# Keeping K and V whole, ordering the loads one by one, and fixing the norm engines in a one-core transformer block

## The chip, the cores and the metric

The kernel runs on one core of one Trainium2 chip. The metric is the device time of one execution in microseconds (us). For a program on one core a run further than 1.5% above the fastest of its kernel counts as slow.

The engines are named as the profile names them: PE is TensorE (matmuls), PEld its weight loads, DVE VectorE, ACT ScalarE, POOL GpSimd, and SP the engine that issues the transfers. "PEclk" is the clock granted to PE as a share of full speed.

## The reference, cut to what matters

A block with conditioning: six modulation vectors come from a small vector `c`, local attention (A) follows a normalization, and a token-mixing MLP (B) follows a second and a third one. S = 2048 tokens, D = 512, 32 heads of 16, a window of 8 keys with dilation 2, F = 1792, all in bf16.

```python
mod = (_silu(c) @ w_mod).reshape(c.shape[0], 6, 1, -1)      # sa, ca, ga, sb, cb, gb
h = _layernorm(x) * (1 + ca) + sa
x = x + ga * _A_ref(h, wqkv, wo)   # q.k over idx = pos - 2*w, w = 0..7; softmax; sum of attn*v; @ wo
h = _layernorm(x) * (1 + cb) + sb
x = x + gb * _B_ref(h, w1, b1, w2, b2)
# _B_ref: h = layernorm(x); u = gelu(einsum('bsd,sf->bdf', h, w1) + b1); y = einsum('bdf,fs->bds', u, w2) + b2
```

## The kernel before

The tokens are split into 16 tiles of 128, and the tiles into five chunks of 2, 4, 4, 4 and 2 tiles (chunks 0 to 4). Each chunk passes through statistics (DVE), normalization, a transpose, the Q, K and V projections (PE), the products Q*K (DVE) with their reduction by matmuls (PE), a softmax, the products with V (DVE), the output projection, two more norms, and then its part of the first MLP matmul. When the last chunk is through, the MLP is finished in a long run of matmuls.

A small scheduler in Python decides the order. Every piece of work is added to a graph with an estimated duration, a rank, and one or more possible engines; the scheduler simulates the engines and emits the instructions in the order of its simulated starts. Because a proxy issues them all, every instruction has the same source line in the profile: L208 in the kernel before, L238 in the changed one. The reader goes by the tile names in the rows.

```python
k_r = ring(NB, [P, 4 * (PAD + CM)], BF, "k_c")     # K of two chunks; PAD = 16 columns are the halo
v_r = ring(NB, [P, 4 * (PAD + CM)], BF, "v_c")
...
if ch:                                             # the halo of K and V is copied from the chunk before
    pC = SIZES[ch - 1] * P
    for nm, cur, r in (("k", k_c, k_r), ("v", v_c, v_r)):
        prev = r[(ch - 1) % NB][:, 0:4 * (PAD + pC)].rearrange("p (j s) -> p j s", j=4)
        copy2(cur[:, :, 0:PAD], lambda prev=prev: prev[:, :, pC:pC + PAD], 4 * PAD, True, ...)
...
# a norm: the scheduler chooses DVE or ACT; the tiles of POOLN1 = (2, 3, 4, 10, 11, 12, 13) go to GpSimd
alts = [("dve", 0.42, lambda: nc.vector.tensor_scalar(dst, src, r_, n_, op0=ALU.mult, op1=ALU.add)),
        ("act", 0.8, lambda: nc.scalar.activation(dst, src, ACT.Identity, scale=r_, bias=n_))]
if pool:
    alts = [("pool", 0.8 if st < 6 else 2.0, lambda: nc.gpsimd.tensor_scalar(...))]
...
# output projection of one tile: the residual x is added by a fifth matmul, with the identity
for dq in range(4):
    nc.tensor.matmul(ps(s_), lhsT=o_sb[:, dq, ...], rhs=woq[:, dq, :], start=(dq == 0), stop=False)
nc.tensor.matmul(ps(s_), lhsT=ident[:], rhs=xx[:, st, :], start=False, stop=True)
...
# products Q*K of one quarter of the head dimension, and their reduction into psL
nc.vector.tensor_tensor(prod, qv, kv, op=ALU.mult)
nc.tensor.matmul(psL[...], lhsT=group4[:], rhs=prod()[...], ...)
```

## Time and profile before

The median was 218.91 us over three runs (218.16 to 219.75), and the profiled execution spans 216.9 us.

| Stage of the kernel before | Time | PE busy | What limits it |
|---|---|---|---|
| 8.00 to 27.09 us | 19.09 us | 11.48 us | loads, GpSimd's norms, VectorE |
| 27.09 to 213.25 us | 186.16 us | 181.67 us | PE itself |

The profile's page of the kernel before, engine totals (busy us, share of the span, instructions) and two rows of its 40 slices (each digit is the busy share of a slice in tenths):

```profile
PE 199.7 (92%) x1450; PEld 99.4 (46%) x1474; DVE 170.1 (78%) x264; ACT 125.9 (58%) x276; POOL 25.9 (12%) x39
...
PE   7776599999999999799998999999999999999993
...
POOL 6025501994000000000000000000000000000000
```

Only the first five slices of PE, and the last, are far from full. In the rest, PE is nearly always busy, so a gain must come from the front, from fewer matmuls, or from the few gaps that are left.

The waits of PE in the kernel before (who was waited for, us in total, times, longest):

```profile
PE psS L208 <- POOL h L208: 2.7, 1, 2.7
PE psS L208 <- DMA wst<-in_w_mod_dram: 1.9, 1, 1.9
PE psS L208 <- DMA h<-in_A_wqkv_dram: 1.6, 1, 1.6
PE psS L208 <- DMA wst<-in_A_wqkv_dram: 1.4, 1, 1.4
```

The timeline of PE in the kernel before, from the last matmuls of chunk 0's projections to chunk 1's first projection (start, us, instruction, count, and in brackets the idle time before it and what ended it):

```profile
14.90 3.66 PE L208 MATMUL psS<-hT,w_qkv 128*128 128x256 bf16 x32
20.41 1.04 PE L208 MATMUL psS<-wst,sc_rep 128*128 128x512 bf16 x3 [1.85 <-DMA wst<-in_w_mod_dram]
...
21.93 0.29 PE L208 MATMUL psS<-ident,h 128*128 128x128 bf16 x2
24.88 0.96 PE L208 MATMUL psS<-ident,h 128*128 128x128 bf16 x14 [2.66 <-POOL h L208]
25.77 0.62 PE L208 MATMUL psL<-big,group 128*32 128x512 bf16 x8
...
27.09 1.03 PE L208 MATMUL psS<-hT,w_qkv 128*128 128x512 bf16 x4
```

The rows `psS<-ident,h` are chunk 1's transposes; they need chunk 1's norms. The row at 27.09 us is chunk 1's first projection (512 columns; chunk 0's have 256), from which on PE is all but full. The same norms on GpSimd, from the timeline of POOL in the kernel before:

```profile
18.45 6.37 POOL L208 TENSOR_SCALAR h<-xx,rs,nb 128x512 bf16<-128x512 bf16 x3 [2.52 <-DVE nb L208]
```

Three norms take 6.37 us there, to 24.8 us (2.73, 0.76 and 2.91 us one by one), and the transposes follow at 24.88. The windows of the kernel before (start:end, length, then busy us and instructions by engine, granted PE clock, share and rate of the transfers):

```profile
8.00:27.09 19.09, 11.48 (x145) 9.02 (x143) 13.84 (x30) 9.76 (x24) 7.83 (x5) 1.00 0.99 299
27.09:213.25 186.16, 181.67 (x1222) 84.03 (x1242) 152.59 (x224) 112.75 (x247) 14.34 (x4) 1.00 0.72 142
```

### The profile page before, as it was taken

How to read it: one execution, taken by the hardware profiler on the slowest of the kernel's cores; microseconds unless marked ns; L12 is line 12 of the kernel's file. 1: busy time of each engine (PE TensorE's matmuls, PEld its weight loads, DVE VectorE, ACT ScalarE, POOL GpSimd, SP SyncE). 2: the span in 40 equal slices, each digit the busy share in tenths (PEclk: the TensorE clock that was granted, in tenths of full speed). 3: DMA queues.
4: the chain of work that ended last, by engine and by line, in shares of the span. 5: the costliest groups of instructions: out<-in, count | busy, mean ns of one | idle time of the engine just before them, and what ended most of it. 6: DMA issues, size and time to landing. Idle time of an engine off the chain costs nothing.

```text
span 216.9 us, 3882 instructions
## 1 busy us (share of the span) xinstructions
PE 199.7 (92%) x1450; PEld 99.4 (46%) x1474; DVE 170.1 (78%) x264; ACT 125.9 (58%) x276; POOL 25.9 (12%) x39
## 2 busy tenths in 40 slices
PE   7776599999999999799998999999999999999993
PEld 7764344445444437433443333444444444444452
DVE  3579599999999899999999989998853455445553
ACT  3637489867897969988887757978753000000000
POOL 6025501994000000000000000000000000000000
PEclk9999999999999999999999999999999999999999
DMA  6999734499999999999989771997169201111111
GB/s 191 350 350 284 232 90 101 79 328 125 165 135 128 136 134 209 154 151 171 188 173 313 225 204 47 284 294 201 50 172 227 66 33 48 53 48 36 36 48 50
DMA packets 53127, 34.24 MB, mean 158 GB/s; under 512 B 18421, under 2 KB 52597, under 8 KB 53109
## 3 DMA queue, kind: packets, MB, share of 16 engines
q1 hardware_dynamic: 53100, 34.00, 72.7%
q8 instruction: 11, 0.18, 0.4%
q14 instruction: 8, 0.06, 0.1%
q10 hardware_dynamic: 8, 0.00, 0.0%
HBM read 22.03 MB, written 2.10 MB: 111 GB/s over the span
## 4 chain that ended last, share of the span: by engine, by line
PE 50%; DMA 14%; issue 8%; POOL 8%; SPq 6%; DVE 6%; ACT 4%; POOLq 2%; ACTq 0%
PE psS L208 50%; POOL h L208 7%; DMA vD<-v_c 7%; SPq L208 6%; DMA h<-in_A_wqkv_dram 5%; DVE big L208 3%; DMA wst<-in_B_w_dram 3%; POOLq L1028 2%; DVE h L208 2%; DVE st L208 1%; ACT junk L208 1%; ACT h L208 1%; ACT k_c L208 0%; ACT o_sb L208 0%; DVE mv L208 0%
## 5 line engine op out<-in xcount | busy, mean ns | idle before, releaser
L208 PE MATMUL psS<-h,wst 128*128 128x512 bf16 x216 | 51.5, 379 | 1.4 <-DMA wst<-in_B_w_dram 0.9
L208 PEld LDWEIGHTS <-wst 128*128 128x128 bf16 x324 | 30.1, 99 | 36.3 <-issue 2.0
L208 PE MATMUL psS<-hT,w_qkv 128*128 128x512 bf16 (+1 forms) x233 | 44.9, 337 | 0.4
L208 PEld LDWEIGHTS <-w_qkv 128*128 128x128 bf16 x282 | 29.6, 112 | 21.0 <-issue 3.8
L208 DVE TENSOR_TENSOR big<-q_sb,k_c 128x4096 bf16<-128x4096 bf16 (+1 forms) x20 | 37.6, 1894 | 0.5 <-PE psL L208 0.5
L208 DVE TENSOR_TENSOR big<-a2sb,vD 128x4096 bf16<-128x4096 bf16 (+1 forms) x20 | 36.8, 1860 | 0.2
L208 DVE SCALAR_TENSOR_TENSOR h<-psS,bcol,gb_bc 128x512 f32<-128x512 f32 (+1 forms) x17 | 12.2, 720 | 24.6 <-PE psS L208 23.0
L208 POOL TENSOR_SCALAR h<-xx,rs,nb 128x512 bf16<-128x512 bf16 x7 | 20.7, 2968 | 14.6 <-DVE nb L208 14.6
L208 ACT ACTIVATE h<-xx,nb,rs 128x512 bf16<-128x512 bf16 x25 | 19.4, 807 | 0.3 <-DVE nb L208 0.2
L208 DVE BATCH_NORM_STATS2 st<-xx 128x6 f32<-128x512 bf16 x24 | 16.3, 679 | 3.3 <-DMA xx<-in_A_x_dram 3.3
L208 PE MATMUL psS<-gT,big 128*128 128x512 bf16 x83 | 18.2, 379 | 0.1
L208 PE MATMUL psS<-woq,o_sb 128*128 128x512 bf16 x62 | 16.6, 381 | 0.9 <-ACT o_sb L208 0.8
L208 PE MATMUL psS<-gT,wst 128*128 128x512 bf16 (+1 forms) x82 | 15.2, 343 | 0.1
L208 PEld LDWEIGHTS <-ident 128*128 128x128 bf16 (+1 forms) x145 | 11.6, 113 | 7.4 <-issue 1.9
L208 ACT ACTIVATE gT<-psS 128x512 bf16<-128x512 f32 x22 | 12.1, 593 | 2.7 <-PE psS L208 2.7
L208 PEld LDWEIGHTS <-big 128*128 128x128 bf16 x116 | 9.1, 97 | 9.9
L208 ACT ACTIVATE k_c<-psS 128x512 bf16<-128x512 f32 x16 | 9.6, 598 | 6.5 <-PE psS L208 6.5
L208 DVE TENSOR_TENSOR psS<-psS,gT 128x512 f32<-128x512 f32 x14 | 9.2, 696 | 5.1 <-PE psS L208 5.1
L208 ACT ACTIVATE q_sb<-psS,qvb 128x512 bf16<-128x512 f32 (+1 forms) x20 | 11.7, 607 | 1.2 <-PE psS L208 1.2
L208 ACT ACTIVATE gT<-psS,bcol 128x512 bf16<-128x512 f32 x14 | 9.1, 687 | 5.2 <-DVE psS L208 5.2
L208 ACT ACTIVATE v_c<-psS,qvb 128x512 bf16<-128x512 f32 (+1 forms) x20 | 11.2, 619 | 1.0 <-PE psS L208 0.8
L208 DVE TENSOR_TENSOR h<-h,xx 128x512 bf16<-128x512 f32 (+1 forms) x17 | 11.2, 661 | 0.6
(94 smaller groups left out, 218.4 us busy)
## 6 DMA issues: line engine op xcount, KB each, us to landing
vD<-v_c SPq DMA_DIRECT2D x48, 130.0 KB, 7.5
wst<-in_B_w_dram SPq DMA_DIRECT2D x6, 768.0 KB, 5.3
wst<-in_B_w_dram SPq DMA_DIRECT2D x4, 896.0 KB, 6.7
big<-in_B_w_dram SPq DMA_DIRECT2D x3, 896.0 KB, 7.7
vD<-v_c SPq DMA_DIRECT2D x32, 66.0 KB, 3.5
out_dram<-h SPq DMA_DIRECT2D x15, 128.0 KB, 1.7
xx<-in_A_x_dram SPq DMA_DIRECT2D x3, 512.0 KB, 9.1
gT<-in_w_mod_dram SPq DMA_DIRECT2D x1, 1536.0 KB
```

Source lines behind the costliest of these rows:

```text
L208: r = fn(*a, **k)
L1028: with _tile.TileContext(nc) as tc:
```

## The change

The change has four intents: to have no halo copies (K and V are kept whole, so the halo is simply the columns to the left), to give every load its own rank so that the order follows need, to give every norm of every tile a fixed engine, and to take three residual adds from PE. The scheduler's model was refined too (GpSimd is blocked while VectorE holds a lock, transfers have a latency and a limited queue), which moves many starts.

```diff
-    k_r = ring(NB, [P, 4 * (PAD + CM)], BF, "k_c")
-    v_r = ring(NB, [P, 4 * (PAD + CM)], BF, "v_c")
+    k_f = T([P, 4, PAD + S], BF, "k_f")
+    v_f = T([P, 4, PAD + S], BF, "v_f")
...
-    POOLN1=(2, 3, 4, 10, 11, 12, 13),
-    LN2D=(2, 3, 10, 11, 12, 13, 14, 15),
+    NE=('AADADAPPPAAPPPAP', 'AAAAADDADAPDPAAA', 'DADDDDDDAAAAPDPD'),
+    X1D=(10, 11, 15),
+    LN2D=(10, 11, 12, 14, 15),
...
-    ld_w(1)
-    ld_w(0)
-    ld_x(1)
-    ld_w(2)
+    for t in (1, 0, 2):
+        G.pk = float(R[f"w{t}"])
+        ld_w(t)
+    for ch in range(1, NCH):
+        G.pk = float(R[f"x{ch}"])
+        ld_x(ch)
...
-    dma(rowA, wmod_view[:, :, 3 * D:6 * D], 3 * D * D * 2, [], ["rowA"], "ld_wmod345")
+    for r in range(3):
+        G.pk = float(R[f"wm{r + 3}"])
+        dma(rowA[:, :, r * D:(r + 1) * D], wmod_view[:, :, (r + 3) * D:(r + 4) * D], ..., f"ld_wmod{r + 3}")
...
-        if ch:                                     # the halo copies
-            ...
-                copy2(cur[:, :, 0:PAD], lambda prev=prev: prev[:, :, pC:pC + PAD], 4 * PAD, True, ...)
...
-                nc.tensor.matmul(ps(s_), lhsT=ident[:], rhs=xx[:, st, :], start=False, stop=True)
+                if st not in X1D:
+                    nc.tensor.matmul(ps(s_), lhsT=ident[:], rhs=xx[:, st, :], start=False, stop=True)
+            if st in X1D:
+                add("dve", 0.69, lambda st=st, s_=s_: nc.vector.tensor_tensor(xx[:, st, :], ps(s_), xx[:, st, :], op=ALU.add), ...)
```

In `NE`, each string is one of the three norms, each letter a tile: A is ScalarE, D VectorE, P GpSimd. The lists of instructions of both kernels, compared engine by engine, give: identity matmuls of the residual 16 to 13; x statistics on VectorE 24 to 21; parking casts of the MLP's partial sums on VectorE 6 to 0 and on ScalarE 22 to 28; halo copies on ScalarE 8 to 0; norms on ScalarE 30 to 22 and on GpSimd 7 to 11. The loads now go out in the order x of chunk 0, K's weights, x of chunk 1, the two first blocks of w_mod, V's weights, Q's weights, and the rest; before, both w_mod blocks and K's and Q's weights preceded the x of chunk 1.

## The prediction

> **What bounds it now.** The profiled span is 216.9 us, TensorE (PE) busy 199.7, VectorE 170.1, ScalarE 125.9 (engine totals). The PE timeline splits in two. From 27.1 to 213.3 us PE is all but full: about 3 us idle (gaps at 72, 90 to 92.5, 97 and 117 us). Before 27.1 us it is starved: between 8 and 27 us it is busy 11.5 of 19 us (windows view). The waits view names the causes: GpSimd's norm of chunk 1 (PE 2.7 us; ScalarE waits 3.2 us for the transposes behind it), the loads of w_mod (1.9), of V's weights (1.6) and of Q's (1.4). VectorE is over 95% busy from 30 to 118 us, nearly a second bound; in the last 67 us it is half idle.
>
> **What the change does.**
> 1. Chunk 1's norms leave GpSimd, where three tiles took 6.4 us (18.4 to 24.8 us); two go to ScalarE (0.8 us each), two to VectorE (0.4). The load of x for chunk 1 comes before both w_mod blocks. Chunk 1's transposes should run near 15 us, not 21.9 to 25.8.
> 2. Q's weights come last of the three, about 14 us instead of 10, and five more x statistics (0.8 us each) stand ahead of the first Q*K product on VectorE. I put it at 19 to 20 us (now 17.05). The four products then run without the 2.3 us wait for the maximum.
> 3. PE starts chunk 1's projections at about 25 us instead of 27.1, with two more modulation rows (0.95 us each) done: a lead of 3.5 to 4 us.
> 4. Eight halo copies of 0.26 us go from ScalarE. The instruction lists also show three statistics fewer on VectorE (0.8 each), six parking casts moved to ScalarE (0.67 on VectorE, 0.6 on ScalarE), three residual adds moved from PE (0.216 each, 0.65 in all) to VectorE (0.69 each). VectorE and ScalarE each lose about 3 us after 27 us.
> 5. GpSimd gets 11 norms instead of 7. The Trainium skill ("SBUF — State Buffer", Who interferes with whom) says that a VectorE operation with two SBUF inputs blocks a GpSimd operation reading SBUF; the trace agrees: a norm took 0.76 us at best, 5.97 at worst. Chunks 2 and 3 have room for it; the last tiles could hold the final h3.
>
> **On the critical path:** item 3 whole (PE-bound after it), 0.65 us of matmuls, perhaps 0.5 us of the 3 us idle. ScalarE's and VectorE's 3 us are mostly slack that keeps PE fed. Sum: about 5.2 us.
>
> **Prediction:** 213.7 us, 8 in 10 between 210.0 and 217.5. Faster by over 2% 0.57, within 2% 0.39, slower by over 2% 0.04.
>
> **What would show it.** In the PE timeline, chunk 1's first 512-column projection at 24 to 26 us (27.1 now); no PE wait for GpSimd's norm in the first 30 us; the first Q*K product at 18 to 20.5 us; PE idle under 4 us from there to the last matmul. No halo copies on ScalarE; the tail from the last level's matmuls unchanged, about 68 us.
>
> **What would make it wrong.** Slower: loads landing later than counted (a modulation row between the Q*K reductions then holds PE and psL); GpSimd norms of chunk 2 or of tiles 10, 12, 14 on the critical path; only 3 groups of matmuls follow the last output projection (12 before), so its norms may stall PE before the last level. Faster: Q's weights landing at 12 to 13 us, the 3 us of idle vanishing, or VectorE's relief counting fully, towards 210.

## The result, and the profile after

The changed kernel took 215.92 us (median of 4 runs, 215.62 to 216.15) against 218.86 for the kernel before (4 runs, 218.16 to 219.75). The ratio is 0.9863, with a 95% interval of 0.9824 to 0.9902. A ratio in this document is the mean time of one kernel's fast runs over that of the other's of the same rounds, so it is not quite the ratio of the medians that are quoted. The change gains about 2.9 us or 1.4%: faster, but by less than the 5.2 us predicted, and the class "within 2%" came, to which the prediction gave less than to "faster by over 2%".

The page after, engine totals, two rows of slices and the granted clock:

```profile
PE 201.8 (94%) x1453; PEld 99.9 (47%) x1475; DVE 168.1 (78%) x256; ACT 123.9 (58%) x270; POOL 24.2 (11%) x43
...
PE   7599999899999999999999999988999999999992
...
PEclk9958999999999999999999999999999999999998
```

The front is full now, and PE is busy for 201.8 us instead of 199.7 although it has fewer identity matmuls to do. The clock row explains part of that: in this execution the granted clock fell to one half between about 11 and 18 us, so the same matmuls were counted as busy for longer. The rest can't be read from the totals: a run at full clock with those three matmuls put back (a_x1dve, below) counts 201.4 us, and traces of the changed kernel itself hold 1453 or 1475 matmul records, so some are missing.

The waits of PE after. The 2.7 us for GpSimd's norm and the 1.6 and 1.4 us for weights are gone:

```profile
PE psS L238 <- DVE st L238: 1.5, 1, 1.5
...
PE psS L238 <- POOL h L238: 1.2, 2, 0.6
PE psS L238 <- DMA hT<-h: 0.9, 1, 0.9
...
PE psS L238 <- DMA big<-in_w_mod_dram: 0.6, 1, 0.6
```

The 1.5 us stand at 7.8 to 9.4 us, before the first matmuls with w_mod. They are put down to a statistics instruction that those matmuls do not read; the load of w_mod is the likelier cause, which this view does not show.

The timeline of PE after: first the front, then the largest gaps behind it:

```profile
15.16 1.86 PE L238 MATMUL psS<-ident,h 128*128 128x128 bf16 x16
16.82 5.13 PE L238 MATMUL psS<-hT,w_qkv 128*128 128x256 bf16 x40
21.88 0.40 PE L238 MATMUL psL<-big,group 128*32 128x512 bf16 x4
...
25.78 0.40 PE L238 MATMUL psL<-big,group 128*32 128x512 bf16 x4
26.11 0.23 PE L238 MATMUL psL<-mask,ident 32*32 32x128 bf16 x1
26.26 1.92 PE L238 MATMUL psS<-hT,w_qkv 128*128 128x512 bf16 x8
...
41.36 1.03 PE L238 MATMUL psS<-hT,w_qkv 128*128 128x512 bf16 x3 [0.85 <-DMA hT<-h]
...
143.49 4.91 PE L238 MATMUL psS<-h,wst 128*128 128x512 bf16 x22 [0.58 <-POOL h L238]
148.99 13.11 PE L238 MATMUL psS<-h,wst 128*128 128x512 bf16 x59 [0.60 <-POOL h L238]
```

Chunk 1's transposes run at 15.16 us, not from 21.93 to 25.8. Yet chunk 1's first projection starts at 26.26 us, only 0.83 us earlier than before. What stands between is VectorE's chain. The timeline of DVE after, the four products Q*K of chunk 0:

```profile
20.16 2.36 DVE L238 TENSOR_TENSOR big<-q_sb,k_f 128x2048 bf16<-128x2048 bf16 x2
22.44 0.15 DVE L238 SCALAR_TENSOR_TENSOR nb<-mv,rs 128x4 f32<-128x4 f32 x1
22.51 2.35 DVE L238 TENSOR_TENSOR big<-q_sb,k_f 128x2048 bf16<-128x2048 bf16 x2
```

The first product started at 17.05 us before, as the timeline of DVE in the kernel before has it:

```profile
17.05 1.22 DVE L208 TENSOR_TENSOR big<-q_sb,k_c 128x2048 bf16<-128x2048 bf16 x1
```

It now has five more statistics ahead of it, and the fourth product ends at 24.86 us; PE's last reduction and the mask come at 25.78 and 26.11, and in PE's order the projection stands behind them. GpSimd's waits have moved to the other end. The last two rows of the timeline of POOL after are the third norm of tiles 12 and 14:

```profile
141.36 2.07 POOL L238 TENSOR_SCALAR h<-h,mv,rs 128x512 bf16<-128x512 bf16 x1 [9.86 <-DVE st L238]
146.77 2.17 POOL L238 TENSOR_SCALAR h<-h,mv,rs 128x512 bf16<-128x512 bf16 x1 [3.33 <-ACT rs L238]
```

They end at 143.43 and 148.94 us, and PE resumes at 143.49 and 148.99 after waits of 0.58 and 0.60 us. The windows after:

```profile
8.00:26.26 18.26, 16.12 (x170) 11.76 (x172) 17.60 (x44) 12.07 (x28) 5.18 (x5) 0.81 1.07 306
26.26:210.50 184.24, 179.71 (x1211) 82.67 (x1231) 147.09 (x203) 108.20 (x237) 15.29 (x9) 1.00 0.73 145
```

The last matmul ends at 210.50 us instead of 213.25. The ledger of these 2.75 us, all from the two traces:

| Term | Predicted | Measured |
|---|---|---|
| Chunk 1's first projection earlier | about 2 us (25 instead of 27.1) | 0.83 us (26.26 instead of 27.09) |
| Modulation rows done by then, 8 more matmuls of 0.216 us | 1.9 us | 1.73 us |
| Lead, sum of the two | 3.5 to 4 us | 2.56 us |
| 3 identity matmuls fewer | 0.65 us | 0.65 us |
| PE's other time after the first projection | 0.5 us less | 0.46 us more |
| Sum | about 5.2 us | 2.75 us |

The 0.46 us is what remains: the stretch from the first projection to the last matmul went from 186.16 to 184.24 us, 1.92 us less, although 1.73 + 0.65 = 2.38 us of matmuls had gone from it. Of the 0.46 us, the gaps that the timelines list account for 0.25 us (they sum to 3.10 us before and 3.35 us after); the rest is spread. By the busy sums of the windows PE's idle time there is 4.49 us before and 4.53 after, so how the 0.46 us divides between idle time and longer matmuls stays open.

### The profile page after: what moved, and what is told of

Read it like the earlier page. It is cut to its first block, busy times and chain, and to the rows that moved or that the text cites. A ratio compares the mean times of both kernels' runs of the same rounds, so it can differ in the third digit from the quotient of the medians.

```text
span 214.4 us, 3880 instructions
## 1 busy us (share of the span) xinstructions
PE 201.8 (94%) x1453; PEld 99.9 (47%) x1475; DVE 168.1 (78%) x256; ACT 123.9 (58%) x270; POOL 24.2 (11%) x43
## 4 chain that ended last, share of the span: by engine, by line
PE 73%; DVE 15%; DMA 4%; issue 3%; ACT 1%; POOLq 1%; SPq 1%; DVEq 0%
PE psS L238 69%; DVE st L238 4%; DVE h L238 4%; PE psL L238 4%; DVE big L238 4%; DMA xx<-in_A_x_dram 3%; DMA hT<-h 2%; DVE mv L238 1%; POOLq L1082 1%; DVE xx L238 1%; SPq L238 1%; DVE w_qkv L238 0%; ACT lv L238 0%; ACT o_sb L238 0%; ACT k_f L238 0%
## 5 line engine op out<-in xcount | busy, mean ns | idle before, releaser
L238 PE MATMUL psS<-hT,w_qkv 128*128 128x512 bf16 (+1 forms) x234 | 47.1, 346 | 1.2 <-DMA hT<-h 0.9
L238 DVE TENSOR_TENSOR big<-q_sb,k_f 128x4096 bf16<-128x4096 bf16 (+1 forms) x20 | 36.8, 1859 | 0.2 <-ACT k_f L238 0.2
L238 ACT ACTIVATE gT<-psS 128x512 bf16<-128x512 f32 x28 | 15.9, 591 | 5.2 <-PE psS L238 5.2
L238 DVE BATCH_NORM_STATS2 st<-xx 128x6 f32<-128x512 bf16 x21 | 14.2, 675 | 4.2 <-DMA xx<-in_A_x_dram 4.1
L238 ACT ACTIVATE h<-xx,nb,rs 128x512 bf16<-128x512 bf16 x17 | 13.3, 809 | 1.8 <-DVE nb L238 1.7
L238 POOL TENSOR_SCALAR h<-xx,mv,rs 128x512 bf16<-128x512 bf16 x2 | 4.3, 2132 | 87.5 <-DVE xx L238 87.0
L238 ACT ACTIVATE v_f<-psS,qvb 128x512 bf16<-128x512 f32 (+1 forms) x20 | 11.5, 601 | 1.1 <-PE psS L238 0.7
L238 POOL TENSOR_SCALAR h<-xx,rs,nb 128x512 bf16<-128x512 bf16 x7 | 10.3, 1485 | 15.3 <-DMA woq<-in_A_wo_dram 8.6
L238 ACT ACTIVATE k_f<-psS 128x512 bf16<-128x512 f32 x16 | 9.5, 597 | 4.0 <-PE psS L238 3.7
L238 ACT ACTIVATE lv<-mv,epscol 128x1 f32<-128x1 f32 (+2 forms) x25 | 7.3, 292 | 7.9 <-DVE mv L238 5.7
```

What stands on the lines that cost most here:

```text
L238: r = fn(*a, **k)
```

## The experiments

In each experiment the schedule of the one or the other kernel is computed as it stands, and then named operations are moved in the list or given another engine, so that all else keeps its order. `mv(names, after=x)` moves operations behind x. Every run had 5 rounds beside the kernel before, and every one gave a correct result. The three calls ran on three chips, and the kernel before took 219.93 and 219.91 us in the first two (medians of 11 runs each) and 219.69 us in the third (8 fast runs; with the three slow ones it would be 220.03). The first call held no run of the changed kernel itself; its runs are compared with its own sisters and, in the trace, with the changed kernel's other traces.

### What chunk 1's norms on GpSimd cost the kernel before

The rival theories were that GpSimd's norms held back the front by their whole wait (A), or that behind that wait stood another one that nearly equalled it (B).

```diff
 # kernel before, after scheduling: n1_2, n1_3 and n1_4 are the norms of tiles 2, 3 and 4
+for n in ("n1_2", "n1_3", "n1_4"):
+    N[n].fn = NF[n]                       # VectorE's form instead of GpSimd's
+mv(["n1_2", "n1_3", "n1_4"], after="nb1_1")
```

> The kernel before, with one thing changed: the norms of chunk 1's tiles 2, 3 and 4 run on VectorE (right after their shift is known) instead of GpSimd; the order of everything else is kept. Theory A (the gain of the change is this norm leaving GpSimd): PE's 2.7 us wait before the transposes of chunk 1 goes, chunk 1's first projection starts near 25 us instead of 27.1, and the time falls by 1.5 to 2.5 us, to about 216.9 us. Theory B (the gain comes from the loads' order or from relief later on): less than 0.5 us, over 218.3 us.

It took 219.15 us, ratio 0.9937 (0.9889 to 0.9985): 0.8 us less than the kernel before by the medians; the interval of the ratio runs from 0.3 to 2.4 us. The wait for GpSimd's norm was gone, and of PE's waits in the front the one for w_mod now stood last. The timeline of PE in this run, with chunk 1's first projection:

```profile
21.41 0.61 PE L208 MATMUL psS<-wst,sc_rep 128*128 128x512 bf16 x1 [2.31 <-DMA wst<-in_w_mod_dram]
...
26.73 1.03 PE L208 MATMUL psS<-hT,w_qkv 128*128 128x512 bf16 x4
```

The load of w_mod that PE meets first in its order ended PE's wait at 20.41 us before and at 21.41 us in this run. In this execution the half clock also fell on the stretch from about 21.4 to 24.7 us, as this row of its windows shows (the value 0.50 is the granted clock):

```profile
23.00:24.00 1.00, 1.00 (x9) 0.14 (x8) 0.10 (x2) 0.67 (x2) 0.00 (x0) 0.50 1.00 354
```

So the removal of a 2.66 us wait was worth 0.8 us by the medians, which lies between what the two theories expected, and the interval does not exclude A. In the trace the first projection came just 0.36 us earlier (26.73 instead of 27.09). But there the load of w_mod landed 1.0 us later than in the other trace, and at half clock PE needed 1.81 us from it to the next reduction (21.41 to 23.22) instead of 0.97 (20.41 to 21.38). That one wait had hidden the next is therefore likely but not shown: what the late load and the half clock took of the gain was not separated.

### The same norms put back on GpSimd in the changed kernel

```diff
 # changed kernel, after scheduling
+for n in ("n1_2", "n1_3", "n1_4"):
+    N[n].fn = NF[n]["P"]                  # GpSimd's form
```

> The changed kernel, with the norms of chunk 1's tiles 2, 3 and 4 put back on GpSimd, order kept. Theory A (taking this norm off GpSimd is a needed part of the gain): PE waits about 2 us before the transposes of chunk 1 (15.2 us now), and the time rises by 1.0 to 2.0 us. Theory B (with x loaded early and no two-input VectorE operation beside it, GpSimd's norms take 0.8 us each and hide): under 0.5 us.

> The changed kernel unaltered, as the control for the runs of this call on the same chip. All theories: 1.0 to 1.8% under the kernel before.

The second text belongs to the control: the unaltered changed kernel. It took 215.80 us (ratio 0.9822, 0.9788 to 0.9856); with the norms on GpSimd it was 216.61 us (0.9852, 0.9816 to 0.9887), 0.8 us more. That is less than A's 1.0 to 2.0 us and more than B's 0.5. The timeline of POOL in this run:

```profile
13.19 1.68 POOL L238 TENSOR_SCALAR h<-xx,rs,nb 128x512 bf16<-128x512 bf16 x2
...
15.55 0.79 POOL L238 TENSOR_SCALAR h<-xx,rs,nb 128x512 bf16<-128x512 bf16 x1
```

The three norms took 0.79, 0.90 and 0.79 us here. No product Q*K ran on VectorE beside them. In the kernel before, the two norms beside which products ran took 2.73 and 2.91 us, and the one between them 0.76 us. PE's own rows in the same run:

```profile
16.40 1.68 PE L238 MATMUL psS<-ident,h 128*128 128x128 bf16 x14 [1.08 <-POOL h L238]
17.87 6.20 PE L238 MATMUL psS<-hT,w_qkv 128*128 128x256 bf16 x40
24.00 0.40 PE L238 MATMUL psL<-big,group 128*32 128x512 bf16 x4
...
28.38 1.92 PE L238 MATMUL psS<-hT,w_qkv 128*128 128x512 bf16 x8
```

And the row of the control for which this run has no counterpart:

```profile
41.74 1.03 PE L238 MATMUL psS<-hT,w_qkv 128*128 128x512 bf16 x4 [1.41 <-DMA hT<-h]
```

PE waited 1.08 us for the norms, and then its 40 projection matmuls took 6.20 us, against 4.53 in the control, because the half clock lasted until about 21 us here and until about 17 in the control. The first reduction came 2.3 us late (24.00 against 21.70), but a wait of 1.41 us that the control has at 41.74 us, for chunk 2's transposes, vanished. More than half of the delay was given back: chunk 1's first projection was 2.29 us late (28.38 against 26.09), chunk 2's only 0.82 us (42.56 against 41.74). So PE is not the only limit behind the front: an earlier or later front is in part made up at 41 us, where PE waits for these transfers. How the 0.8 us divides between GpSimd and the clock is not settled: the three runs with a mean clock of 0.983 or 0.984 took 216.34 to 216.55 us, those at 0.976 took 216.66 to 216.99.

### The five statistics ahead of the first product

If VectorE's order limits the front (A), moving three of the five statistics behind the second product should bring 0.5 to 1.0 us. If the loads of the next modulation rows come next (B), it should bring nothing.

```diff
 # changed kernel, after scheduling: ln1s8 to ln1s10 are the statistics of tiles 8 to 10
+mv(["ln1s8", "ln1s9", "ln1s10"], after="qk0_1")
```

> The changed kernel, with three of the five x statistics that stand ahead of the first Q*K product on VectorE moved behind the second one. Theory A (they hold the start of chunk 1's projections, the term of the prediction that came out 1.2 us too large): the first product starts at 18 to 19.4 us instead of 20.2, chunk 1's first projection near 25.3 instead of 26.3, time down by 0.5 to 1.0 us. Theory B (VectorE only does the same work in another order, and the modulation rows between the reductions wait for their w_mod load, about 22 us): the first product is earlier, the first projection stays at 26 us or later, time within 0.3 us.

It took 215.86 us (0.9823, 0.9788 to 0.9858), the same as the control. The timeline of DVE of this run shows that the product did move, to 18.01 us from 20.43 in the control:

```profile
18.01 2.36 DVE L238 TENSOR_TENSOR big<-q_sb,k_f 128x2048 bf16<-128x2048 bf16 x2
```

and the timeline of PE of this run shows why nothing came of it:

```profile
23.38 1.04 PE L238 MATMUL psS<-gT,sc_rep 128*128 128x512 bf16 x4 [1.12 <-DMA gT<-in_w_mod_dram]
...
26.14 1.70 PE L238 MATMUL psS<-hT,w_qkv 128*128 128x512 bf16 x7
```

PE waits for a modulation row's load instead, and the projection starts at 26.14 us (control 26.09). Theory B holds. The front after the change has two limits within a few tenths of a microsecond of each other: VectorE's chain and the loads.

### The halo copies

A: the eight copies were on the way, and putting them back costs up to 2 us. B: ScalarE has slack, and they cost nothing that can be seen.

```diff
 # changed kernel; hk is a spare tile, and the result does not depend on it
+for ch in range(1, NCH):
+    e = T0[ch] * P
+    ins(lambda e=e: nc.scalar.activation(hk[:, 0], k_f[:, :, e:e + PAD], ACT.Identity), before=f"ev{ch}_10")
+    ins(lambda e=e: nc.scalar.activation(hk[:, 1], v_f[:, :, e:e + PAD], ACT.Identity), before=f"ev{ch}_20")
```

> The changed kernel, with eight dummy copies of the halo's size put back on ScalarE (from the kept K and V into a spare tile), one ahead of the first K and one ahead of the first V eviction of chunks 1 to 4. Theory (ScalarE has slack there): under 0.4 us slower. Rival (ScalarE's queue paces the evictions): up to the 2 us that the copies take.

It took 216.32 us (0.9811, 0.9768 to 0.9854). From chunk 2's first projection to PE's last resumption, 41.03 to 148.82 us in this trace, it needed 107.79 us; the changed kernel needs 107.63 (41.36 to 148.99). Six of the eight copies lie in this stretch: about 1.5 us of ScalarE's work cost 0.16 us. The other two lie before it, where the wait for chunk 2's transposes (1.11 us here) varies among runs of the unaltered kernel from 0.85 to 1.41 us, more than they could show. The median is 0.2 to 0.5 us above those of the changed kernel, on other chips. As work of ScalarE, the copies that give the change its name are worth next to nothing by themselves; that K and V no longer wait for them was not tested, since nothing depends on the dummies.

### The residual adds on VectorE

If the three identity matmuls (0.65 us) count in full, putting them back costs that much (A). The rival expected less, or even a gain when ScalarE does the copy, because VectorE would be relieved.

```diff
 # changed kernel; the identity matmul comes back for tiles 10, 11 and 15
-                if st not in X1D:
+                if True:
                     nc.tensor.matmul(ps(s_), lhsT=ident[:], rhs=xx[:, st, :], start=False, stop=True)
 # and the sum is copied by VectorE (first run) or by ScalarE (second run)
-  nc.vector.tensor_tensor(xx[:, st, :], ps(s_), xx[:, st, :], op=ALU.add)
+  nc.vector.tensor_copy(xx[:, st, :], ps(s_))                           # a_x1dve
+  nc.scalar.activation(xx[:, st, :], ps(s_), ACT.Identity)              # a_x1act
```

> The changed kernel, with the residual add of tiles 10, 11 and 15 back on PE (identity matmul), and VectorE only copying the sum out of PSUM, at the same cost as its add. Theory as predicted (PE-bound, 0.65 us of matmuls saved): the time rises by 0.65 us, to 216.6 us. Rival (the saved matmuls fall where PE waits 1.2 us for the norms of the last tiles anyway): no rise over 0.2 us, and the PE waits near 143 and 149 us shrink instead.

> As the run above, but ScalarE copies the sum out, as before the change, so VectorE loses three instructions of 0.69 us. Rival theory (VectorE, busy without a gap from 124 to 148 us, sets when the last tiles' norms are done): the time falls by 0.3 to 1.0 us, to about 215.2 us, and the final norm of tile 15 (149.1 us now) comes 0.7 us or more earlier. Theory as predicted: it rises by 0.65 us, to 216.6 us.

With VectorE's copy it took 216.19 us (0.9805, 0.9761 to 0.9849). From the reduction after the gap at about 97 us to PE's last resumption the stretch is 52.56 us (97.19 to 149.75) against 52.34 us (96.65 to 148.99) in the changed kernel: only 0.22 of the 0.65 us is seen, because the waits before the tail shrank (0.37 us for GpSimd's norm instead of 0.58, 0.20 us instead of 0.41 for a product). With ScalarE's copy it took 216.95 us (0.9834, 0.979 to 0.9879), 0.76 us more than with VectorE's; the stretch was 53.28 us, and PE waited 0.67 us at 133.99 us for a product. So the part of the rival theory that expected ScalarE's copy to be faster fell. Where on ScalarE the copy lost its time was not tested further. For the time, the engine of the add matters here more than the matmul that it saves.

The first of these runs had full clock throughout its profile, which tells whether the half clock in the front cost the changed kernel anything. Its timeline of PE:

```profile
21.79 0.40 PE L238 MATMUL psL<-big,group 128*32 128x512 bf16 x4 [2.13 <-DVE big L238]
...
26.31 1.92 PE L238 MATMUL psS<-hT,w_qkv 128*128 128x512 bf16 x8
```

At full clock PE was done early and waited 2.13 us for VectorE's first product; the projection began at 26.31 us, against 26.26 at half clock. The half clock only filled a wait there.

### An early load that holds up a transpose

The waits of the changed kernel show 0.85 us, in the controls 1.41 and 1.20 us, for chunk 2's transposes, which are transfers issued by SP. The queue of SP is busy without a gap at that time, and the load of the first MLP weights stands ahead.

```diff
 # changed kernel, after scheduling
+mv(["ld_w1_0_0"], before="ld_w1_0_512")
```

> The changed kernel, with the first load of B_w1 (768 KB, issued at 24.5 us, needed at 92 us) moved from ahead of chunk 0's copies of V to just before the next load of B_w1. Theory: the queue is busy without a gap from 25 to 62 us, so all behind it comes 0.6 us or more earlier; PE's wait of 0.85 us for the transposes of chunk 2 (41 us) and VectorE's of 1.55 us for the copies of V (39 us) shrink by half or more; time down by 0.4 to 1.0 us. Rival (those waits are made up later, or PE waits for B_w1 at 92 us instead): within 0.3 us, or slower.

It took 216.00 us (0.981, 0.9775 to 0.9846), with a mean 0.25 us below the control's. The wait for the transposes disappeared, as PE's row at this place shows; a shorter one for the V eviction is left:

```profile
41.21 1.03 PE L238 MATMUL psS<-hT,w_qkv 128*128 128x512 bf16 x4 [0.46 <-ACT v_f L238]
```

VectorE's wait for the copies of V, which was to shrink too, did not: its product started at 40.79 us here and in the control. The gain is too small to tell from nothing with these runs. It is inconclusive.

### Three attempts at a faster version

The last call held a second control and three builds: the reduction of chunk 4's last product moved ahead (a_red), this with the later load (a_best2), and these with the front reordered so that chunk 1's projections come between the reductions (a_best).

```diff
 # a_red: changed kernel, after scheduling
+mv(["red4_3"], after="qk4_3")
+mv(["sub4"], after="wo10")
 # a_best2 = a_red and
+mv(["ld_w1_0_0"], before="ld_w1_0_512")
 # a_best = a_best2 and
+mv(["ln1s8", "ln1s9", "ln1s10"], after="qk0_1")
+mv(["qkv1_10"], after="red0_0")
+mv(["ev1_10"], after="ev0_22")
+mv(["qkv1_00", "ev1_00"], after="red0_1")
+mv(["modrow0", "ga_bc"], after="red0_2")
+mv(["exp0", "modrow2", "ab_bc", "modrow1", "sb_bc"], after="sub0")
+mv(["woq_s"], after="qk1_0")
```

> The changed kernel unaltered, the control of this call. All theories: 215.5 to 216.6 us, 1.2 to 1.9% under the kernel before.

> The changed kernel, with two short PE steps of the last chunk earlier in PE's order: its last Q*K reduction one group of MLP matmuls earlier, the subtraction of its maximum one output projection earlier. Theory (VectorE's work after that reduction, without a gap from 124 to 148 us, sets the norms for which PE waits 0.6 us at 143 and 0.6 us at 149): VectorE's 1.5 us wait for the maximum shrinks by about 0.9 us, the last norm (149.1 us) comes 0.7 to 0.9 us earlier, time down by 0.5 to 0.9 us. Rival (ScalarE's short steps pace that chain): the last norm moves by less than 0.3 us, time within 0.3 us.

> The run above and the late load of B_w1 together. Theory (they act at 41 and at 149 us, both on PE's order, so they add): 0.8 to 1.4 us under the control. Rival: no more than the run above alone.

> The run above, with three statistics behind the second Q*K product, the first two projections of chunk 1 set between the Q*K reductions, and the modulation rows moved behind them, with what follows from them. Theory (once the statistics are out of the way, only the w_mod rows in PE's order hold PE there): PE's wait for w_mod goes, PE has the first two projections and a row done 0.8 to 1.5 us sooner, and the time falls by a further 0.3 to 1.0 us. Rival (the wait comes back at 41 us for the transposes of chunk 2, whose queue starts no earlier): within 0.3 us of the run above.

The control took 216.13 us (0.9849, 0.981 to 0.9888). a_red took 217.09 us (0.9894, 0.9855 to 0.9932), 1.0 us more than the control. It was built wrongly, and does not test its theory as it was meant: moving the subtraction placed it ahead of the maximum in the list, so the maximum had to wait for the subtraction, and the subtraction used an old maximum. (The result stayed correct, since a softmax does not depend on the value subtracted.) It does show something by accident: it delays the last maximum. The maximum in the timeline of DVE of the control, and then of a_red:

```profile
123.91 0.69 DVE L238 TENSOR_REDUCE m<-psL 128x64 bf16<-128x512 f32 x1 [1.49 <-PE psL L238]
```

```profile
125.08 0.69 DVE L238 TENSOR_REDUCE m<-psL 128x64 bf16<-128x512 f32 x1 [2.97 <-PE psL L238]
```

Measured from the reduction at about 97 us, the maximum came 1.49 us later (28.33 instead of 26.84 us) and PE's last resumption 1.13 us later (53.47 instead of 52.34). New waits of PE make up that time: 0.46 us at 122.17 us for the product itself, whose reduction now stands too early, and 0.67 us at 130.05 us for the softmax behind the maximum. So PE does not absorb a delay of that chain, which has little slack. Whether an earlier maximum would gain anything was not shown, since the run that should have tested it was built wrongly.

a_best2 took 216.82 us (0.9885, 0.9842 to 0.9928), 0.27 us below a_red; that is again not separable, and it inherits the fault. a_best took 219.25 us (0.9995, 0.9952 to 1.0039), 2.4 us more than a_best2. Its projections did start early, at 21.55 us, but the timeline of DVE shows this row ahead of chunk 1's first product:

```profile
31.36 0.19 DVE L238 COPY bcol<-psS 128x30 f32<-128x30 f32 x1 [2.86 <-ACT gb_bc L238]
```

VectorE stood for 2.86 us at a copy of 0.19 us whose input was late. The moves had changed PE's and ScalarE's order but left this copy where it was in VectorE's queue. PE had two new waits, 1.47 us for the maximum at 27.73 us and 1.49 us at 35.27 us. No version beat the changed kernel.

## Why the prediction was right or wrong, point by point

1. *"Chunk 1's transposes should run near 15 us."* Right: 15.16 us. No PE wait for a norm on GpSimd is left in the first 30 us, as predicted.
2. *"I put it [the first product] at 19 to 20 us."* It was 20.16 us, 0.16 us past its upper end, and within the 18 to 20.5 us that the prediction named as its sign.
3. *"A lead of 3.5 to 4 us"*: mis-sized; it measured 2.56 us. The mechanism was right, including the additional modulation rows. The step that failed is "about 25 us" for the projection: it was 26.26 us. The four products take 4.70 us from the first start to the last end, and PE's wind-up (the last reduction and the mask) stands between them and the projection, which began 1.40 us after the fourth product's end. They took 6.10 us together, so the prediction's own range for the first product, 19 to 20 us, would have given 25.1 to 26.1 us; it took the lower end. The prediction probably also credited the removal of GpSimd's wait too highly: in the kernel before, taking it away alone gave 0.8 us by the medians, of a 2.66 us wait (b_norm1; the interval reaches 2.4 us). And VectorE's order is not the only limit: with the first product at 18.01 us the loads held the projection at 26.14 us (a_stats). The words "item 3 whole (PE-bound after it)" failed as well: 0.85 us of the lead went at 41 us into the wait for chunk 2's transposes, and a front that was 2.29 us late cost only 0.82 us behind that place (a_norm1).
4. *"0.65 us of matmuls"*: the three matmuls are gone (0.65 us of work), but put back together with a VectorE copy they cost only 0.22 us of the measured stretch; the rest comes back as shorter waits (a_x1dve).
5. *"Perhaps 0.5 us of the 3 us idle"*: wrong in sign. PE's other time after the first projection grew by 0.46 us. Most of the old gaps did go, but new ones came: 0.85 us for a transpose, and 0.58 and 0.60 us for the tail norms of tiles 12 and 14 on GpSimd. The prediction named the tail norms as a risk, and did not cost them.
6. *"ScalarE's and VectorE's 3 us are mostly slack."* Right for ScalarE's halo copies (a_halo: 0.16 us for about 1.5 us of work). For VectorE the runs are narrower: early statistics in the front had slack (a_stats), while its chain before the tail had little (a_red).
7. The predicted time, 213.7 us, was 2.2 us too low, and the range held the result, because it was 7.5 us wide. Points 3 and 5 are the two terms that were too favourable: about 1.2 us and 1.0 us. Their sizes are read from one trace of each kernel.

Open: the gain was 2.9 us in the first comparison, and 4.1 and 3.6 us in the later calls with a control (medians of fast runs). The changed kernel stayed within 215.8 to 216.1 us in all of them; the kernel before moved from 218.9 to 219.9 us. The two slowest of its fast runs, 222.11 and 222.06 us, had the lowest mean clock, 0.966, but fast runs at 0.984 range from 217.69 to 220.14 us, so the clock alone doesn't explain it, and only the profiled execution shows where in time the clock was low. Open too: no run put the old order of the loads back alone. That this order made the largest term of the ledger possible, the 1.73 us of modulation rows done in the front, is read from the traces and not shown by an experiment.

## What to carry to other kernels

A wait that the profile shows is not yet what its removal brings: before counting it, ask which wait stands next in the same engine's order, and when that one would end (here about 0.8 us came of a 2.66 us wait, and nothing of a product moved 2.4 us ahead). Work taken from an engine that was not the limit, the halo copies on ScalarE, gave next to nothing here, however visible it is in the lists of instructions. When a stage is started earlier, follow its last input, through every instruction queued ahead of it on each engine, before putting a start time on it.

## What the Trainium skill lacked or had wrong

- "SBUF — State Buffer", section "Who interferes with whom": the rule that a VectorE operation with two SBUF inputs blocks a GpSimd operation reading SBUF agrees with the runs: two norms beside the products took 2.73 and 2.91 us, the one between them 0.76 us, and three without products (a_norm1) 0.79 to 0.90 us. What the page lacks is the size for such a pair; here it is a factor of about 3.7, and the longest norm of the kernel before, in chunk 3, took 5.97 us. The same section's other rule, that single-input VectorE operations in the two-port modes block or are blocked in their turn, shows on VectorE's side: with GpSimd normalizing beside them (a_norm1) four scalings took 2.08 us, and 1.13 us in the control. No view names the mode of these scalings, so this is a likely reading and not a shown one.
- "TensorE: Matmul & The Clock Gate", Part 1: The HAM clock gate, gives half clock after an idle window of about 3.4 us, with a phase that differs from run to run. The trace agrees with the half (0.50 granted from 12 to 18 us) and with the variation (mean clock 0.98 to 1.00 in four runs of the changed kernel). What it does not say is how busy a window may be and still count as idle: PE was busy for 1.09 us between 8 and 11 us, before the clock fell. Nor does it say when the half clock matters: it cost nothing where PE waited anyway (26.26 us at half clock, 26.31 at full), and 1.67 us over 40 matmuls where PE was the limit (6.20 against 4.53 us).
- How long a transfer holds the queue that issues it, none of the pages that I read gives for transposes of this size on this chip. In the changed kernel's trace a transpose of one 128x512 tile held SP's queue for about 1.2 us and one of the V copies for 0.65 us.
